# A small tile behind the others in its pool, and three pieces of a matmul stage in another order on the engines

## The chip, the cores and the metric

The kernel runs on one core of one Trainium2 chip. The time is device time of one launch in microseconds (us), the median of several runs. Five engines work side by side: PE (TensorE, matmuls; its weight loads are shown as PEld), DVE (VectorE), ACT (ScalarE), POOL (GpSimd) and SP, which here only issues DMAs.

## The reference

Three pieces follow one another. Attention over pooled keys and values gives 4608 tokens of 512 features; a gated layer (1536 wide) gives 4608 x 512 again; the last one, the **rational stage**, is the one that is changed:

```python
h = x @ w_in                                  # 4608x512 @ 512x2048
P = a[0] + a[1]*h + a[2]*h**2 + a[3]*h**3
Q = 1.0 + abs(b[0])*abs(h) + abs(b[1])*h**2
g = P / (Q + 1e-06)
return g @ w_out                              # 4608x2048 @ 2048x512
```

Everything is fp32. A product of two fp32 matrices is made of three matmuls on "high" and "low" parts (high x high, low x high, high x low).

## The kernel before

**Tiling.** The tokens are cut into 9 blocks of 512. The 2048 hidden columns are taken 256 at a time: a **couple** `n` is one block `j` and one of its 8 pairs `c` of 128 columns, so there are 72 couples (`TOTAL`), `n = 8j + c`. For a couple PE makes `z` (the hidden values, two PSUM banks of 128x512: `z_gv`, the left half, and `z_at`, the right half), ACT and DVE turn `z` into `g = P/Q`, and 24 matmuls of 128x512 (`out2`, profile line L1217, tile `acco`) add `g @ w_out` into four result banks, one for each 128 tokens. Here `g` is the stationary operand, loaded 128x128 at a time, and a tile of `w_out` (`wo`) moves.

**Two ways to make z.** Blocks 0 to 2 (couples 0 to 23, "plain") use 24 matmuls of 128x512 (`whole`, L262). Blocks 3 to 8 ("seven") use a seven-product scheme with 42 matmuls of 128x256 (`product`, L1182), spread over two turns of the loop (`begin7`).

**From z to g.** For a half (or for both halves at once, `all_`) the steps are: `look` (three ACT reads of z: L1252, L1255, L1258), `denominator` (DVE, L1272), `inverse` (ACT, Ln and Exp: L1278, L1279), `poly` (two DVE operations that read z again: L1267, L1268; after them the bank of z is free), `quotient` (DVE, L1283, L1284), `finish` (DVE, L1288), `high` (ACT rounds to the high part of g, L1308) and `low` (the low part of g, on POOL at L1317 or on DVE at L96). `g` stands in tiles `g0` (high) and `g1` (low), three buffers each.

**Order.** The order on each engine is that of the code; nothing is rescheduled. Turn `n` of the loop makes z of couple `n`, does the second part of the chain for couple `n-1`, and issues `outputs(n-3, 1)` and later `outputs(n-2, 0)`: result rows 2, 3 of couple `n-3`, and rows 0, 1 of couple `n-2`. Couple 0 and the last one, 71, are carried through the chain in one go by `alone(n)`. A waiting instruction holds what stands behind it on its engine.

**Banks and tiles.** z has two `gv` and two `at` banks, so z of couple `n` waits for `poly` of couple `n-2`. The result banks are the four of a ring: a block's results are copied out by `leave2` to a tile `ob` (two buffers) and sent with a DMA: row 0 (DVE), row 1 and row 3 (ACT) in turn `c == 2` of the next block, row 2 (DVE) in turn `c == 3`. The block's new rows 2 and 3 are begun in that same turn.

**The pool.** SBUF tiles of the stage come from a pool `p2`, one after another in the order in which the code first asks for them. The first is

```python
turn_ = p2.tile([P, 8], F32, name="turn")
```

32 bytes in a partition; it is written by a one-column copy on POOL that only keeps POOL in its place in the order. Behind it stand `sq`, `w0`, `t`, `g0`, `g1`, `ob`, `cq`, whose sizes are whole multiples of 1024 bytes. In the built program the first buffer of `g` begins at byte 198432 of a partition (32 above a multiple of 64), as all of `p2` behind `turn` does; the weights of all other 128x512 matmuls begin at multiples of 64.

Of the kernel before, what the change touches and what calls it, by code (L numbers as in the profile page):

```python
# [10 lines left out]
F32 = mybir.dt.float32  # L11
# [8 lines left out]
P = 128  # L20
# [4 lines left out]
DM = H * D  # L25
# [4 lines left out]
BLK = 512  # L30
# [36 lines left out]
def attention_gated_rational(  # L67
# [4 lines left out]
    nc = tc.nc  # L72
# [1056 lines left out]
    with tc.tile_pool(name="p2", bufs=1, reuse_waits="tile") as p2:  # L1129
# [11 lines left out]
        def seven(n):  # L1141
            return n // NC2 >= PLAIN2
# [25 lines left out]

        def zbanks(n):
            zs[n] = [  # L1170
                pool.tile([P, BLK], F32, tag=tag, name=f"z{n}_{tag}") for pool, tag in ((ps_gv, "gv"), (ps_at, "at"))
            ]

        Q_C11, Q_C12, Q_C21, Q_C22 = range(4)
# [33 lines left out]
        def out2(n, half):  # L1208
            j, c = divmod(n, NC2)
            if c == 0:  # L1210
                for i in (0, 1) if half == 0 else (2, 3):
                    accs[j, i] = chain_bank(f"acco{j}_{i}")
            gt = gts[n]
            for i in (0, 1) if half == 0 else (2, 3):
                for m, (lw, rw) in enumerate(((0, 0), (1, 0), (0, 1))):
                    for f in range(2):
                        nc.tensor.matmul(  # L1217
                            accs[j, i], gts[n][lw][:, f * BLK + i * P : f * BLK + (i + 1) * P],
                            W2[f"o2_{2 * c + f}"][:, rw, :],
                            start=c == 0 and m == 0 and f == 0, stop=c == NC2 - 1 and m == 2 and f == 1,  # L1220
                        )
            if half:
                gts.pop(n)

        def leave2(n, i, eng=None):
            j, c = divmod(n, NC2)
            if n < 0 or c < NC2 - 1:
                return
            ob = p2.tile([P, DM], F32, tag="ob", name=f"ob{j}_{i}", bufs=2)
            if eng is None:  # L1230
                nc.scalar.activation(ob, accs[j, i], AF.Copy)
            else:
                eng.tensor_copy(ob, accs[j, i])  # L1233
            r0 = j * BLK + i * P
            nc.sync.dma_start(out[r0 : r0 + P, :], ob)
# [29 lines left out]
        def poly(n, c):  # L1265
            t, z = tiles[n]["t"][:, c], zs[n][c.start // BLK]
            nc.vector.tensor_tensor(t, t, z, op=ALU.mult)  # L1267
            nc.vector.scalar_tensor_tensor(t, t, neg[:, 1:2], z, op0=ALU.add, op1=ALU.mult)  # L1268

        def denominator(n, c):  # L1270
            sq, w0 = tiles[n]["sq"][:, c], tiles[n]["w0"][:, c]
            nc.vector.scalar_tensor_tensor(w0, sq, neg[:, 5:6], w0, op0=ALU.mult, op1=ALU.add)  # L1272
# [14 lines left out]
            e, t = (tiles[n][k][:, c] for k in ("e", "t"))  # L1287
            nc.vector.scalar_tensor_tensor(e, t, neg[:, 0:1], e, op0=ALU.add, op1=ALU.mult)  # L1288

        def alone(n):  # L1290
            denominator(n, left)
            inverse(n, left)
            if not seven(n):
                poly(n, left)
            denominator(n, right)
            inverse(n, right)
            poly(n, right)
            quotient(n, left)
            finish(n, left)
            high(n, left)  # L1300
            quotient(n, right)
            finish(n, right)
            high(n, right)
            low(n, left)
            low(n, right)

        def high(n, c):
# [81 lines left out]

        counts = {}  # L1390
        sums2 = {}

        def sum_begin(n):
            c = n % NC2
# [31 lines left out]
        for n in range(EARLY2):  # L1426
            stream2(n)
        left, right = cols[True]
        turn_ = p2.tile([P, 8], F32, name="turn")

        def outputs(n, half):
            if 0 <= n < TOTAL:
# [2 lines left out]
        for n in range(TOTAL):  # L1435
            after = n + 1 if n + 1 < TOTAL and seven(n + 1) else None
            j, c = divmod(n, NC2)
            chain_tiles(n)
            x_load(n)
            if seven(n):  # L1440
                product(n, Q_C11, "a12", "b21")
                product(n, Q_C12, "s4", "b22")
                product(n, Q_C21, "s3", "t3")
                stream2(n + 2, 0, 1)
                add7(n, Q_C22)
                look(n, left)
                if seven(n - 1):
                    inverse(n - 1, all_)
                poly(n, left)
            else:  # L1450
                whole(n, 0)
                look(n, left)
                whole(n, 1)
                sum_begin(n)
                held.pop(n)
                stream2(n + EARLY2, *((0, 1, 3, 2) if seven(n + EARLY2) else ()))
            leave2(n - 3, 0, nc.vector)
            leave2(n - 4, 2, nc.vector)
            if after:
                begin7(after)  # L1460
            leave2(n - 3, 1)
            if seven(n):
                x_high(n, X_HIGH[c])
            elif j + 1 < PLAIN2:
                if "x" in box:
                    box.pop("x")()
            else:
                x_do(n, X_POOL[c], nc.vector)
                x_do(n, X_DVE[c], nc.vector)
            sum_low(n)  # L1470
            if n > 1:
                quotient(n - 1, all_)
            outputs(n - 3, 1)
            if seven(n):
                product(n, Q_C21, "a22", "t4")
                held.pop(n)
                stream2(n + 2, 3)
            if after:
                product(after, Q_C21, "s2", "t2")
                if seven(n):  # L1480
                    stream2(n + 2, 2)
            if n > 1:
                finish(n - 1, all_)
            if after:
                add7(after, Q_C12)
            look(n, right)
            if n > 1:
                high(n - 1, left)
                high(n - 1, right)
            if n == 0:  # L1490
                alone(n)
            elif n == TOTAL - 1:
                low(n - 1, all_, nc.gpsimd)
                alone(n)
            elif seven(n):
                poly(n, right)
                if X_POOL[c] and j + 1 < NB:
                    nc.gpsimd.tensor_copy(turn_[:, :1], tiles[n - 1]["e"][:, :1])  # L1498
                    x_do(n, X_POOL[c], nc.gpsimd)
                x_do(n, X_DVE[c], nc.vector)  # L1500
                denominator(n, all_)
                nc.gpsimd.tensor_copy(turn_[:, :1], tiles[n]["w0"][:, :1])  # L1502
                low(n - 1, all_, nc.gpsimd)
            else:
                denominator(n, all_)
                if n > 1:
# [12 lines left out]
            outputs(n - 2, 0)  # L1519
# [63 lines left out]
```

## Time and profile before

| | |
|---|---|
| three runs | 1759.24, 1759.27, 1761.99 us; median 1759.27 |
| the profiled execution | 1762.16 us; its span, first to last instruction, 1760.3 us |
| PE busy | 1720.0 us (98%) |
| weight loads (PEld) busy | 1441.5 us (82%) |
| DVE, ACT, POOL busy | 1357.8 (77%), 1156.6 (66%), 590.1 us (34%) |
| the rational stage | from 974.92 us to the end |

Busy shares tell how much an engine had to do; since PE's matmuls overlap one another, 98% does not mean that PE could not go faster. What sets the time is read from the order of events: which engine waits for which.

### The profile page before, as it was taken

The page shows a single profiled execution, that of the slowest core. Times are in us where ns is not written, and L with a number is a line of the kernel's source. Part 1 is how long each engine was busy: PE and PEld are TensorE (multiplying, and loading weights), DVE is VectorE, ACT ScalarE, POOL GpSimd, SP SyncE. Part 2 cuts the span into 40 slices and gives each one's busy share as a digit, 9 for nine tenths or more (in the row PEclk, how much of TensorE's full clock was granted, in tenths as well). Part 3 has the DMA queues.
Part 4 walks back from the last instruction along what each step waited for, and adds up shares of the span by engine and source line. Part 5 has one row for each costly group of instructions (what it writes and reads, how often), then busy time and mean ns, then how long its engine had stood idle before and what let it go on. Part 6 is the DMA issues. An engine that isn't in the chain of part 4 may idle for free.

```text
span 1760.3 us, 26293 instructions
## 1 busy us (share of the span) xinstructions
PE 1720.0 (98%) x9040; PEld 1441.5 (82%) x9040; DVE 1357.8 (77%) x2030; ACT 1156.6 (66%) x1980; POOL 590.1 (34%) x685
## 2 busy tenths in 40 slices
PE   6999999999999999999999999999999999999998
PEld 5777787788777888788888788888888888898887
DVE  7996767678677664387777799997888888888887
ACT  6785557577577654355545677776677777777775
POOL 3443334344635532100000164542343333333321
PEclk9999999999999999999999999999999999999999
DMA  7833767889999999994527545445446464555540
GB/s 286 296 137 135 252 250 247 314 327 379 380 325 356 335 335 354 386 394 168 192 80 255 192 168 191 168 156 202 154 165 254 154 233 172 218 191 198 190 176 25
DMA packets 173924, 413.11 MB, mean 235 GB/s; under 512 B 16864, under 2 KB 71008, under 8 KB 172768
## 3 DMA queue, kind: packets, MB, share of 16 engines
q1 hardware_dynamic: 172928, 410.85, 64.3%
q8 instruction: 72, 1.18, 0.3%
q10 hardware_dynamic: 864, 0.60, 0.1%
q14 instruction: 60, 0.49, 0.1%
HBM read 307.57 MB, written 103.81 MB: 234 GB/s over the span
## 4 chain that ended last, share of the span: by engine, by line
PE 82%; DVE 7%; ACT 5%; issue 2%; POOL 2%; DMA 1%; POOLq 0%; SPq 0%; DVEq 0%; ACTq 0%
PE acco L1217 22%; PE ca L262 10%; PE z_at L1182 9%; PE ya L1110 7%; PE cc L262 5%; PE z_gv L1182 4%; PE yc L1110 4%; PE z_gv L262 3%; PE z_at L262 3%; PE vp L262 3%; PE gp L262 3%; PE cb L262 2%; PE yb L1110 2%; PE pv L463 2%; PE sc L374 1%
## 5 line engine op out<-in xcount | busy, mean ns | idle before, releaser
L1217 PE MATMUL acco<-wo,g 128*128 128x512 f32 x1728 | 423.7, 395 | 3.8 <-DVE ob L1233 2.9
L1217 PEld LDWEIGHTS acco<-wo,g 128*128 128x128 f32 x1728 | 317.1, 188 | 75.3 <-DVE ob L1233 5.6
L1317 POOL TENSOR_TENSOR g<-e,g 128x512 fp32r<-128x512 f32 x140 | 190.3, 1381 | 390.1 <-PE z_at L262 284.8
L1252 ACT ACTIVATE t<-z_gv,neg 128x512 f32<-128x512 f32 x72 | 56.0, 777 | 100.7 <-PE z_gv L1182 73.4
L1272 DVE SCALAR_TENSOR_TENSOR w<-sq,neg,w 128x1024 f32<-128x1024 f32 (+1 forms) x74 | 95.1, 1286 | 21.1 <-ACT w L1258 21.1
L1283 DVE SCALAR_TENSOR_TENSOR e<-w,sq 128x1024 f32<-128x1024 f32 (+1 forms) x74 | 92.1, 1244 | 24.9 <-ACT sq L1279 22.3
L1308 ACT ACTIVATE g<-e 128x512 fp32r<-128x512 f32 x144 | 83.6, 630 | 41.3 <-DVE e L1288 40.6
L262 PE MATMUL vp<-x,wv 128*128 128x512 f32 x432 | 109.8, 402 | 0.7 <-DVE wv L96 0.4
L262 PE MATMUL gp<-x,wg 128*128 128x512 f32 x432 | 106.8, 394 | 1.4 <-DVE wg L96 0.9
L1288 DVE SCALAR_TENSOR_TENSOR e<-t,neg,e 128x1024 f32<-128x1024 f32 (+1 forms) x74 | 95.8, 1295 | 2.6
L262 PEld LDWEIGHTS gp<-x,wg 128*128 128x128 f32 x432 | 79.8, 188 | 20.4 <-DVE wg L96 2.9
L262 PEld LDWEIGHTS vp<-x,wv 128*128 128x128 f32 x432 | 80.1, 190 | 19.5 <-DVE wv L96 2.8
L1284 DVE SCALAR_TENSOR_TENSOR e<-e,sq 128x1024 f32<-128x1024 f32 (+1 forms) x74 | 91.9, 1241 | 2.5
L1252 ACT ACTIVATE t<-z_at,neg 128x512 f32<-128x512 f32 x72 | 56.2, 781 | 49.6 <-PE z_at L1182 37.9
L1279 ACT ACTIVATE sq<-sq,lnb 128x1024 f32<-128x1024 f32 (+1 forms) x74 | 83.6, 1130 | 2.4
L1278 ACT ACTIVATE sq<-w 128x1024 f32<-128x1024 f32 (+1 forms) x74 | 77.1, 1042 | 9.2 <-DVE w L1272 8.9
L1267 DVE TENSOR_TENSOR t<-t,z_gv 128x512 f32<-128x512 f32 x72 | 49.3, 685 | 32.6 <-ACT w L1258 32.6
L126 POOL TENSOR_TENSOR rawo<-rawo 128x256 uint32<-128x256 uint32 (+1 forms) x41 | 32.0, 781 | 120.1 <-issue 34.6
L941 DVE TENSOR_TENSOR cc<-cq,ca 128x512 f32<-128x512 f32 x36 | 25.0, 694 | 59.9 <-PE ca L262 59.9
L1502 POOL COPY turn<-w 128x1 f32<-128x1 f32 x47 | 8.7, 185 | 162.9 <-DVE w L1272 152.4
L262 PE MATMUL z_gv<-z,y 128*128 128x512 f32 x252 | 60.8, 390 | 1.5 <-DVE t L1268 1.5
L1498 POOL COPY turn<-e 128x1 f32<-128x1 f32 x35 | 6.5, 185 | 165.6 <-DVE e L1288 165.6
(361 smaller groups left out, 4433.8 us busy)
## 6 DMA issues: line engine op xcount, KB each, us to landing
y<-s2d SPq DMA_DIRECT2D x98, 512.0 KB, 4.9
y<-i_parts SPq DMA_DIRECT2D x91, 512.0 KB, 5.9
sw<-sd SPq DMA_DIRECT2D x72, 512.0 KB, 6.9
sw<-wd SPq DMA_DIRECT2D x36, 512.0 KB, 6.7
h<-hq SPq DMA_DIRECT2D x36, 512.0 KB, 6.8
y<-i_parts SPq DMA_DIRECT2D x49, 256.0 KB, 3.2
sd<-ws SPq DMA_DIRECT2D x24, 512.0 KB, 3.2
hl<-h SPq DMA_DIRECT2D x24, 512.0 KB, 6.7
```

Source lines behind the costliest of these rows:

```text
L262: nc.tensor.matmul(acc, st[:, lw, cols], mv[:, rw, mcols], start=first and i == 0, stop=last and i == n - 1, skip_group_check=seeded,)
L1110: nc.tensor.matmul(banks[q], w[:, lw, cols], t[:, rw, :], start=opened and k == 0 and m == 0, stop=k == NK - 1 and m == 2, skip_group_chec ...
L1182: nc.tensor.matmul(zpart(n, q), w[:, lw, (2 * k + i) * P : (2 * k + i + 1) * P], t[rw][i], start=first and m == 0, stop=m == 5, skip_group ...
L1217: nc.tensor.matmul(accs[j, i], gts[n][lw][:, f * BLK + i * P : f * BLK + (i + 1) * P], W2[f"o2_{2 * c + f}"][:, rw, :], start=c == 0 and m ...
L1252: nc.scalar.activation(tiles[n]["t"][:, c], zs[n][c.start // BLK], AF.Identity, scale=neg[:, 3:4], bias=neg[:, 2:3])
L1272: nc.vector.scalar_tensor_tensor(w0, sq, neg[:, 5:6], w0, op0=ALU.mult, op1=ALU.add)
L1279: nc.scalar.activation(ln, ln, AF.Exp, scale=-1.0, bias=lnb)
L1283: nc.vector.scalar_tensor_tensor(e, w0, C1, ln, op0=ALU.add, op1=ALU.mult)
L1284: nc.vector.scalar_tensor_tensor(e, e, 2.0, ln, op0=ALU.subtract, op1=ALU.mult)
L1288: nc.vector.scalar_tensor_tensor(e, t, neg[:, 0:1], e, op0=ALU.add, op1=ALU.mult)
L1308: nc.scalar.activation(gts[n][0][:, c], tiles[n]["e"][:, c], AF.Copy)
L1317: eng.tensor_tensor(lo[:, h], e[:, h], f32(hi[:, h]), op=ALU.subtract)
```

## The change

Four edits, all in the rational stage.

1. The 32-byte tile `turn` is asked for when it is first used, and so stands behind all other tiles of `p2`. In the built program the first buffer of `g` then begins at byte 198400, a multiple of 64.
2. Start: couple 0 puts its left half into an `at` bank and its right half into a `gv` bank. `alone(0)` is gone: couple 0 gets `denominator`, `inverse` and both `poly` in its own turn, and the second part of its chain in turn 1, behind couple 1's `look`.
3. The copy of result row 2 (`leave2(n-4, 2)`) goes ahead of `poly(n, left)` on DVE.
4. End: `last_couple` takes the place of `alone(71)`; it weaves the second part of couple 70's chain into that of couple 71, with `low(70)` on DVE. In all couples the matmuls with the low part of `g` come last of the three; in couple 71 all rows take the left half of g first, then the right. The last four results leave through four tiles.

```diff
-                pool.tile([P, BLK], F32, tag=tag, name=f"z{n}_{tag}") for pool, tag in ((ps_gv, "gv"), (ps_at, "at"))
+                pool.tile([P, BLK], F32, tag=tag, name=f"z{n}_{tag}")
+                for pool, tag in ((ps_gv, "gv"), (ps_at, "at"))[:: 1 if n else -1]
...
-            for i in (0, 1) if half == 0 else (2, 3):
-                for m, (lw, rw) in enumerate(((0, 0), (1, 0), (0, 1))):
-                    for f in range(2):
...
+            rows = (0, 1) if half == 0 else (2, 3)
+            steps = [(i, m, f) for i in rows for m in range(3) for f in range(2)]
+            if n == TOTAL - 1:
+                steps = [(i, m, half) for i in range(4) for m in range(3)]
+            for i, m, f in steps:
+                lw, rw = ((0, 0), (0, 1), (1, 0))[m]
...
+            if n < TOTAL - 1:
+                ob = p2.tile([P, DM], F32, tag="ob", name=f"ob{j}_{i}", bufs=2)
+            else:
+                ob = p2.tile([P, WIDE], F32, tag=("sq", "w0")[i // 2], name=f"ob{j}_{i}", bufs=2)[:, :DM]
...
+        def last_couple(n):
+            look(n, right)
             inverse(n, left)
+            for h in (left, right):
+                finish(n - 1, h)
+                high(n - 1, h)
             denominator(n, right)
             inverse(n, right)
+            for h in (left, right):
+                low(n - 1, h)
             quotient(n, left)
             finish(n, left)
             high(n, left)
+            poly(n, right)
+            low(n, left)
             quotient(n, right)
             finish(n, right)
             high(n, right)
-            low(n, left)
             low(n, right)
...
-        turn_ = p2.tile([P, 8], F32, name="turn")
...
+        def turn(src):
+            if not turns:
+                turns.append(p2.tile([P, 8], F32, name="turn"))
+            nc.gpsimd.tensor_copy(turns[0][:, :1], src[:, :1])
...
                 add7(n, Q_C22)
+                leave2(n - 4, 2, nc.vector)
                 look(n, left)
...
                 poly(n, left)
+                if n == TOTAL - 1:
+                    denominator(n, left)
...
-            leave2(n - 4, 2, nc.vector)
...
-            if n > 1:
-                quotient(n - 1, all_)
+            if n == 1:
+                look(n, right)
+            if n > 0:
+                for h in (left, right) if n == 1 else (all_,):
+                    quotient(n - 1, h)
+                    if n == 1:
+                        finish(n - 1, h)
...
             if n == 0:
-                alone(n)
+                for h in (left, right):
+                    denominator(n, h)
+                    inverse(n, h)
+                poly(n, left)
+                poly(n, right)
             elif n == TOTAL - 1:
-                low(n - 1, all_, nc.gpsimd)
-                alone(n)
+                last_couple(n)
```

**Start, DVE.** These are DVE's rows for couple 0 and the first of couple 1, before (`w`, `t`, `e`, `g` are the tiles of the chain; the first numbers of a couple's tiles are 95xx and 96xx).

```order
L1272 SCALAR_TENSOR_TENSOR w_9586<-sq_9585,neg,w_9586 128x512
L1267 TENSOR_TENSOR t_9587<-t_9587,z_gv 128x512
L1268 SCALAR_TENSOR_TENSOR t_9587<-t_9587,neg,z_gv 128x512
L1272 SCALAR_TENSOR_TENSOR w_9586<-sq_9585,neg,w_9586 128x512
L1267 TENSOR_TENSOR t_9587<-t_9587,z_at 128x512
L1268 SCALAR_TENSOR_TENSOR t_9587<-t_9587,neg,z_at 128x512
...
L1288 SCALAR_TENSOR_TENSOR e_9629<-t_9587,neg,e_9629 128x512
L96 SCALAR_TENSOR_TENSOR g_9628<-e_9629,g_9627 128x512 x2
L1272 SCALAR_TENSOR_TENSOR w_9650<-sq_9649,neg,w_9650 128x1024
```

And of the change:

```order
L1277 SCALAR_TENSOR_TENSOR w_9585<-sq_9584,neg,w_9585 128x512 x2
L1272 TENSOR_TENSOR t_9586<-t_9586,z_at 128x512
L1273 SCALAR_TENSOR_TENSOR t_9586<-t_9586,neg,z_at 128x512
L1272 TENSOR_TENSOR t_9586<-t_9586,z_gv 128x512
L1273 SCALAR_TENSOR_TENSOR t_9586<-t_9586,neg,z_gv 128x512
...
L1293 SCALAR_TENSOR_TENSOR e_9628<-t_9586,neg,e_9628 128x512
L1277 SCALAR_TENSOR_TENSOR w_9639<-sq_9638,neg,w_9639 128x1024
L96 SCALAR_TENSOR_TENSOR g_9627<-e_9628,g_9626 128x512 x2
```

Both denominators now stand ahead of both polynomials, and couple 1's denominator ahead of couple 0's low part. On ACT, `high` of couple 0 moved from before the six reads of couple 1's z to behind them.

**A block's fourth turn, DVE** (the one of block 3; `ob_2` is the copy of result row 2), before:

```order
L1206 TENSOR_TENSOR z_at<-cq_11959,z_at 128x256
L1267 TENSOR_TENSOR t_12029<-t_12029,z_gv 128x512
L1268 SCALAR_TENSOR_TENSOR t_12029<-t_12029,neg,z_gv 128x512
L1233 COPY ob_2_12063<-acco_2_11274 128x512
L1283 SCALAR_TENSOR_TENSOR e_12058<-w_11907,sq_11906 128x1024
```

And of the change:

```order
L1207 TENSOR_TENSOR z_at<-cq_11959,z_at 128x256
L1238 COPY ob_2_12053<-acco_2_11273 128x512
L1272 TENSOR_TENSOR t_12029<-t_12029,z_gv 128x512
L1273 SCALAR_TENSOR_TENSOR t_12029<-t_12029,neg,z_gv 128x512
L1288 SCALAR_TENSOR_TENSOR e_12061<-w_11907,sq_11906 128x1024
```

The copy moved up past two operations. This is so at six places, in blocks 3 to 8; in blocks 1 and 2 nothing stood between on DVE, and its rows are as before.

**The end, DVE** (tiles 16xxx and 17034, 17035 are couple 70's, 17009, 17010 and higher couple 71's), before:

```order
L1288 SCALAR_TENSOR_TENSOR e_17035<-t_16910,neg,e_17035 128x1024
L1272 SCALAR_TENSOR_TENSOR w_17009<-sq_17008,neg,w_17009 128x512 x2
L1267 TENSOR_TENSOR t_17010<-t_17010,z_at 128x512
L1268 SCALAR_TENSOR_TENSOR t_17010<-t_17010,neg,z_at 128x512
L1283 SCALAR_TENSOR_TENSOR e_17071<-w_17009,sq_17008 128x512
...
L1288 SCALAR_TENSOR_TENSOR e_17071<-t_17010,neg,e_17071 128x512
L96 SCALAR_TENSOR_TENSOR g_17070<-e_17071,g_17069 128x512 x2
```

And of the change:

```order
L1293 SCALAR_TENSOR_TENSOR e_17035<-t_16910,neg,e_17035 128x512 x2
L1277 SCALAR_TENSOR_TENSOR w_17009<-sq_17008,neg,w_17009 128x512
L96 SCALAR_TENSOR_TENSOR g_17034<-e_17035,g_17033 128x512 x2
L1288 SCALAR_TENSOR_TENSOR e_17066<-w_17009,sq_17008 128x512
L1289 SCALAR_TENSOR_TENSOR e_17066<-e_17066,sq_17008 128x512
L1293 SCALAR_TENSOR_TENSOR e_17066<-t_17010,neg,e_17066 128x512
L1272 TENSOR_TENSOR t_17010<-t_17010,z_at 128x512
L1273 SCALAR_TENSOR_TENSOR t_17010<-t_17010,neg,z_at 128x512
L96 SCALAR_TENSOR_TENSOR g_17065<-e_17066,g_17064 128x512
```

Couple 70's low part came to DVE (POOL loses its two last subtractions), couple 71's left denominator went up in front of couple 70's quotient, and couple 71's right polynomial moved behind its left quotient.

## Rows read from the trace of the kernel before

**Rows 1.** Chain that ended last, merged: start us, us, engine, tile, line, count

```profile
843.67 8.16 PE yc L1110 x36
...
1009.91 2.73 PE z_at L262 x12
1012.63 5.59 PE acco L1217 x24
...
1023.68 5.59 PE acco L1217 x24
...
1248.72 2.79 PE acco L1217 x12
...
1259.30 2.79 PE acco L1217 x12
1270.64 2.79 PE acco L1217 x12
```

**Rows 2.** Busy us by stretch of one couple: PE, PEld, DVE, ACT, POOL, clock, DMA

```profile
1023.67:1034.72 11.05, 11.05 (x50) 9.02 (x49) 10.95 (x11) 7.14 (x12) 9.04 (x7) 1.00 0.29 118
...
1200.39:1211.44 11.05, 11.05 (x50) 9.01 (x49) 8.82 (x10) 7.47 (x11) 3.10 (x2) 1.00 0.15 51
```

**Rows 3.** What PE waited for in the rational stage: us, times, longest

```profile
PE acco L1217 <- DVE ob L1233: 2.9, 6, 0.5
```

**Rows 4.** Timeline at the stage's start: start us, us, [idle before <-releaser]

```profile
974.92 3.02 PE L262 MATMUL z_gv<-z,wi 128*128 128x512 f32 x12 [0.69 <-ACT yq L1079]
...
982.58 0.75 DVE L1272 SCALAR_TENSOR_TENSOR w<-sq,neg,w 128x512 f32<-128x512 f32 x1 [0.59 <-ACT w L1258]
...
985.94 2.88 PE L262 MATMUL z_gv<-z,wi 128*128 128x512 f32 x12
...
989.51 0.76 ACT L1252 ACTIVATE t<-z_gv,neg 128x512 f32<-128x512 f32 x1
...
991.38 2.96 PE L1217 MATMUL acco<-wo,g 128*128 128x512 f32 x12
...
993.11 1.28 DVE L1272 SCALAR_TENSOR_TENSOR w<-sq,neg,w 128x1024 f32<-128x1024 f32 x1 [2.77 <-ACT w L1258]
...
995.83 3.03 PE L262 MATMUL z_gv<-z,y 128*128 128x512 f32 x12 [1.49 <-DVE t L1268]
```

**Rows 5.** Timeline, fourth turn of block 3

```profile
1265.43 0.69 DVE L1267 TENSOR_TENSOR t<-t,z_gv 128x512 f32<-128x512 f32 x1 [0.73 <-ACT w L1258]
1265.51 1.56 PE L1217 MATMUL acco<-wo,g 128*128 128x512 f32 x6
...
1266.82 0.68 DVE L1233 COPY ob<-acco 128x512 f32<-128x512 f32 x1
...
1267.56 1.66 PE L1217 MATMUL acco<-wo,g 128*128 128x512 f32 x6 [0.49 <-DVE ob L1233]
```

**Rows 6.** The tile ob: its DMAs, from issue to landing

```profile
DMA to landing us min/median/max: 2.0/2.1/5.9
```

**Rows 7.** Timeline at the end

```profile
1737.92 1.23 DVE L1283 SCALAR_TENSOR_TENSOR e<-w,sq 128x1024 f32<-128x1024 f32 x1 [0.66 <-ACT sq L1279]
1737.92 6.84 PE L1217 MATMUL acco<-wo,g 128*128 128x512 f32 x27
1738.12 0.78 ACT L1252 ACTIVATE t<-z_at,neg 128x512 f32<-128x512 f32 x1 [0.24 <-PE z_at L1182]
...
1742.47 2.98 POOL L1317 TENSOR_TENSOR g<-e,g 128x512 fp32r<-128x512 f32 x2 [5.57 <-ACT g L1308]
...
1744.35 1.65 DVE L1283 SCALAR_TENSOR_TENSOR e<-w,sq 128x512 f32<-128x512 f32 x1
...
1745.50 10.77 PE L1217 MATMUL acco<-wo,g 128*128 128x512 f32 x45 [0.74 <-POOL g L1317]
...
1747.42 0.68 DVE L1283 SCALAR_TENSOR_TENSOR e<-w,sq 128x512 f32<-128x512 f32 x1
...
1756.35 0.69 DVE L1233 COPY ob<-acco 128x512 f32<-128x512 f32 x1 [2.16 <-PE acco L1217]
```

More of the change, by code (lines that the diff above doesn't have):

```diff
@@ L1212, in out2 @@
                     accs[j, i] = chain_bank(f"acco{j}_{i}")
-            gt = gts[n]
-            for i in (0, 1) if half == 0 else (2, 3):
-                for m, (lw, rw) in enumerate(((0, 0), (1, 0), (0, 1))):
-                    for f in range(2):
[L1217 to L1221, printed above, removed]
+            rows = (0, 1) if half == 0 else (2, 3)
[4 more added lines that the diff above has]
+                lw, rw = ((0, 0), (0, 1), (1, 0))[m]
+                nc.tensor.matmul(
+                    accs[j, i], gts[n][lw][:, f * BLK + i * P : f * BLK + (i + 1) * P], W2[f"o2_{2 * c + f}"][:, rw, :],
+                    start=c == 0 and m == 0 and f == 0, stop=c == NC2 - 1 and m == 2 and f == 1,
+                )
             if half:
@@ L1228, in leave2 @@
                 return
-            ob = p2.tile([P, DM], F32, tag="ob", name=f"ob{j}_{i}", bufs=2)
+            if n < TOTAL - 1:
+                ob = p2.tile([P, DM], F32, tag="ob", name=f"ob{j}_{i}", bufs=2)
+            else:
+                ob = p2.tile([P, WIDE], F32, tag=("sq", "w0")[i // 2], name=f"ob{j}_{i}", bufs=2)[:, :DM]
             if eng is None:
@@ L1288, in finish @@
             nc.vector.scalar_tensor_tensor(e, t, neg[:, 0:1], e, op0=ALU.add, op1=ALU.mult)
-        def alone(n):
-            denominator(n, left)
+        def last_couple(n):
+            look(n, right)
             inverse(n, left)
-            if not seven(n):
-                poly(n, left)
+            for h in (left, right):
+                finish(n - 1, h)
+                high(n - 1, h)
             denominator(n, right)
             inverse(n, right)
-            poly(n, right)
+            for h in (left, right):
+                low(n - 1, h)
             quotient(n, left)
@@ L1391, in attention_gated_rational @@
         sums2 = {}
+        turns = []
+        def turn(src):
+            if not turns:
+                turns.append(p2.tile([P, 8], F32, name="turn"))
+            nc.gpsimd.tensor_copy(turns[0][:, :1], src[:, :1])
         def sum_begin(n):
@@ L1449, in attention_gated_rational @@
                 poly(n, left)
+                if n == TOTAL - 1:
+                    denominator(n, left)
             else:
                 whole(n, 0)
+                leave2(n - 4, 2, nc.vector)
                 look(n, left)
@@ L1481, in attention_gated_rational @@
                     stream2(n + 2, 2)
-            if n > 1:
+            if 1 < n < TOTAL - 1:
                 finish(n - 1, all_)
@@ L1485, in attention_gated_rational @@
                 add7(after, Q_C12)
-            look(n, right)
-            if n > 1:
+            if 1 != n < TOTAL - 1:
+                look(n, right)
+            if 0 < n < TOTAL - 1:
                 high(n - 1, left)
@@ L1497, in attention_gated_rational @@
                 if X_POOL[c] and j + 1 < NB:
-                    nc.gpsimd.tensor_copy(turn_[:, :1], tiles[n - 1]["e"][:, :1])
+                    turn(tiles[n - 1]["e"])
                     x_do(n, X_POOL[c], nc.gpsimd)
@@ L1501, in attention_gated_rational @@
                 denominator(n, all_)
-                nc.gpsimd.tensor_copy(turn_[:, :1], tiles[n]["w0"][:, :1])
+                turn(tiles[n]["w0"])
                 low(n - 1, all_, nc.gpsimd)
@@ L1505, in attention_gated_rational @@
                 denominator(n, all_)
-                if n > 1:
+                if n == 1:
+                    low(n - 1, left)
+                    low(n - 1, right)
+                else:
                     low(n - 1, all_, nc.gpsimd)
```

## The prediction

> **What bounds the kernel now.** I read the chain of waits first, then busy time by stretch, then what PE waited for, and last the order of events at the three places that the change touches. In the rational stage the chain is PE nearly without a break, and each plain couple follows the last after 1023.68 - 1012.63 = 11.05 us, in which PE has no gap [rows 1]. A heavy couple (DVE 10.95 us, POOL 9.04) and a light one (DVE 8.82, POOL 3.10) take the same 11.05 us at the same granted clock of 1.00 [rows 2]. So the other engines only matter where PE waits for one: the reader should see three such places, the first couples, the six block changes, and the last two couples. All else must come from the pace of the matmuls themselves.
>
> That pace is not one number. 36 matmuls of the layer before take 8.16 us, 226.7 ns each; 12 for z take 2.73 us, 227.5 ns; but 24 of `acco` take 5.59 us, 232.9 ns [rows 1]. All are 128x512 of the same type, in the same couple as the z ones, and neither the clock nor the neighbours' load differs [rows 2]. What I see that differs is the place of the stationary operand: g starts 32 bytes above a multiple of 64, all other such weights at one.
>
> **Edit 1, the small tile.** It moves g by 32 bytes and adds no instruction; the other tiles of the pool move too, on engines that PE doesn't wait for. The trace before has no `acco` matmul with g at a multiple of 64, so the price is bounded: nothing at the one end; at the other the pace of the neighbours, 5.59 - 24 x 0.2267 = 0.15 us a couple, over 72 couples 10.8 us. I take the upper end, because every 512-column group whose weights start at a multiple of 64 runs near 227 ns and the only one that doesn't runs at 233. Why 32 bytes should cost this no row tells; it is a coincidence of two facts that I take for a cause.
>
> The Trainium skill speaks against it: its page "SBUF — State Buffer", section "Specifications (TRN2)", gives SBUF lines of 16 bytes and a penalty for crossing to a new one. 32 is a whole number of such lines, so by that rule g was as well placed before as after, and edit 1 is worth nothing. The same page says in "Operand start alignment" that its alignment runs timed nothing. No run here yet shows which holds; the sum by that rule is the first rival below.
>
> **Edit 2, the start.** Before, z of couple 0 waits 0.69 us for the copy of the last `ya` out of the `gv` bank. With the left half in `at` it starts at 974.2; the right half needs that bank 2.7 us later. Next, couple 3's z starts at 995.83, 1.49 us late by the profile, for couple 1's polynomial; couple 1's reads began only at 989.51, since ACT stood behind couple 0's `high`, and DVE idled 2.77 us before couple 1's denominator at 993.11 [rows 4]. After: couple 0's right denominator at 981.85 (0.7 earlier than 982.58), then four polynomial operations at about 0.72 each, so the `gv` bank that couple 2 wants is free at 985.4, half a microsecond ahead of 985.94. Couple 2's 24 matmuls end at 990.9. DVE meanwhile runs without a gap: six operations for quotient and finish of couple 0 to 989.8, couple 1's denominator (1.28) to 991.1, two low parts to 992.5, couple 1's left polynomial to 994.0. PE's 12 matmuls of couple 0's rows start at 990.9, need the low part 1.1 us in, wait some 0.4 us, and end at 994.0. Couple 3's z starts there: 995.83 - 994.0 = **1.8 us**. Bounds: 0.7 (the bank alone) and 2.4 (no new wait). DVE has come forward by about as much, so the lead lasts.
>
> **Edit 3, row 2's copy.** Couples of the seven-product part follow one another after 1259.30 - 1248.72 = 10.58 us, but over the block change 1270.64 - 1259.30 = 11.34 [rows 1]: 0.76 us more, at six block changes 4.5 us. The cause stands in the rows: after six matmuls from 1265.51 the bank of the next row is still being copied, from 1266.82 to 1267.50 [rows 5], and the waits list the same copy six times [rows 3]. In its new place DVE meets the copy at about 1264.7, in the 0.73 us for which it idles for ACT's reading [rows 5]; the copy takes 0.68. So it is hidden, ends 1.5 us before PE asks, and the polynomial behind it is at most some hundredths late. Without that cover it would cost 0.68 us of DVE, on which PE doesn't wait there. Gain **4.5 us**; the lower bound is the idle time as recorded, 2.9 [rows 3].
>
> **Edit 4, the end.** From 1737.92 PE has 27 matmuls at 0.233, 6.29 us, then should go on at 1744.21; it goes on at 1745.50, having waited for POOL's low part of couple 70 (from 1742.47 for 2.98 us) [rows 7]. That is 1.3 us. After it the last 45 run through. In the new order, from DVE's 1737.92: couple 70's quotient 2.5 us, then fifteen operations of 0.72 (0.68 by the row at 1747.42, and the step to the next): finish twice, denominator, low part of 70 at the fifth (1744.0), quotient, finish, polynomial and low part left at the eleventh (1748.3), low part right at the fifteenth, some 1752.0 with its wait for ACT's rounding. POOL no longer works beside DVE, which had stretched one of these to 1.65 us [rows 7]. PE at 226.7 ns asks for these at 1744.3, 1749.3 and 1752.0: in time, the last by a hair. The order of the three terms alone (low last) only gives each low part two more matmuls of time. So 1.3 us; against it the four results come out 0.68 us apart instead of 1.4, and four transfers of 256 KB that land after 2.1 us when alone [rows 6] may queue: 0.2 us by guess. Gain **1.1 us**, bounds 0.3 and 1.6. The copy and the DMA behind the last matmul (1756.35 to the end) stay.
>
> **Sum.** 10.8 + 1.8 + 4.5 + 1.1 = 18.2 us. The profiled execution took 1762.16 (span 1760.3), so one like it would take 1744.0, with a span of 1742.1. The median run was 2.9 us shorter than the profiled one; from 1759.27 the forecast is **1741.1 us**, about 1.0% faster.
>
> **Rivals.**
> First, the pace stays: what slows `acco` is something that the change keeps, such as g having been written only just before by ACT and POOL, or two tiles of w_out by turns. Against it: z and the layer before also go through several moving tiles, and the pace is the same beside idle and busy neighbours. It is what the page's rule would give. Time: 1759.27 - 7.4 = 1751.9.
> Second, DVE takes PE's place as the bound in the plain blocks: a couple there would have 11.05 - 0.15 = 10.90 us and the heaviest DVE row is 10.95 [rows 2]. Light couples between give it back; if the gain of edit 1 were lost in all of the first 16 couples, 2.4 us, the time would be 1743.5.
> Third, slower: the copy of row 2 waits for its buffer of `ob`, that is, for the landing of row 1's DMA, and now holds the polynomial, and with it z's bank, behind it. It stands some 6.7 us after that DMA's issue; the longest landing was 5.9 [rows 6]. Beyond 6.7 each microsecond costs one at each of six places; to end 0.2% above before, landings would have to pass 10.3 us, a wait of 3.62 us six times, 21.7 against the 18.2 gained: 1762.8.
> That the change doesn't do what it says is no rival here: the order on the engines and the place of g are those of the built program.
>
> **How the numbers follow.** Forecast 0.74, with a range of its own from 1740.0 (start and end at their upper bounds, 19.3 us gained) to 1745.7 (edit 1 at 90%, the other three at their lower bounds, 13.6 gained). Pace stays 0.15; DVE the bound 0.04; edit 1 in part, between the first two, 0.02; the late landing 0.05, of which 0.02 costs enough to end above before by 0.2% and 0.03 eats the gain only. The range of 1739.0 to 1752.5 leaves a microsecond under the forecast's best case and takes in the first rival's centre, without which a fifth of the chance would hang on one unproved cause. A run of this kernel tells 0.2% (3.5 us) from no change; faster by more has 0.95, within it 0.03, slower 0.02.
>
> **What would show it.** In the chain, 24 `acco` matmuls should take 5.44 us, plain couples follow after 10.90 and the others after 10.43, block changes too. If 5.59 stays, edit 1 was worth nothing. No wait of `acco` for `ob` should be left; couple 3's z should start near 994.0; behind the last z PE should run 72 matmuls with no gap over 0.1 us. I am wrong if PE shows new waits for a polynomial or a low part, above all in blocks 0 to 2, or if the last DMA lands much more than 2.2 us after its issue.

## The result, and the profile after

| | before | after |
|---|---|---|
| median | 1759.26 us (1759.05 to 1761.99, 4 runs) | 1745.26 us (1744.37 to 1747.41, 4 runs) |
| the profiled execution, its span | 1762.16, 1760.3 us | 1747.41, 1745.6 us |

The ratio is 0.9919, with a 95% interval of 0.9901 to 0.9936: 14.0 us less by the medians, where 18.2 were forecast. The time lies inside the range given, 4.2 us above the forecast's 1741.1. Between the two profiled executions, which the rest of this section compares, it is 14.7 us.

The chain of waits of the kernel after, in the plain blocks and in block 3 (start us, us, engine, tile, line, count):

```profile
988.08 2.72 PE z_at L262 x12
...
1009.92 5.44 PE acco L1220 x24
1020.80 5.44 PE acco L1220 x24
...
1242.74 2.75 PE acco L1220 x12
...
1253.26 2.75 PE acco L1220 x12
...
1263.78 2.75 PE acco L1220 x12
```

Read it against [rows 1]. The 24 `acco` matmuls take 5.44 us where they took 5.59, so they run at the pace of their neighbours, and a plain couple follows the last after 1020.80 - 1009.92 = 10.88 us. In the seven-product blocks a group of 12 takes 2.75, not 2.79, and a couple 1253.26 - 1242.74 = 10.52 us, block changes (1253.26 to 1263.78) too. The forecast had 10.43 there.

All that PE and its weight loads still wait for in the stage (us, times, longest); the first row is at couple 2's z, the second in couple 0's result rows:

```profile
PEld z_gv L262 <- DVE t L1273: 0.5, 1, 0.5
PEld acco L1220 <- DVE g L96: 0.2, 1, 0.2
```

The wait of `acco` for `ob` [rows 3] is gone. DVE is busy nearly throughout a heavy plain couple and PE still does not wait for it (busy us by stretch: PE, PEld, DVE, ACT, POOL, clock, DMA):

```profile
1023.36:1034.24 10.88, 10.88 (x49) 9.01 (x48) 10.74 (x11) 6.95 (x12) 9.29 (x6) 1.00 0.08 31
```

The three places in the timeline, in order (start, block 3's fourth turn, end):

```profile
973.96 2.88 PE L262 MATMUL z_at<-z,wi 128*128 128x512 f32 x12
...
993.42 2.90 PE L262 MATMUL z_gv<-z,y 128*128 128x512 f32 x12
...
1258.54 0.68 DVE L1238 COPY ob<-acco 128x512 f32<-128x512 f32 x1
...
1259.44 2.91 PE L1220 MATMUL acco<-wo,g 128*128 128x512 f32 x12
...
1724.34 16.51 PE L1220 MATMUL acco<-wo,g 128*128 128x512 f32 x72
...
1737.09 0.69 DVE L96 SCALAR_TENSOR_TENSOR g<-e,g 128x512 fp32r<-128x512 f32 x1 [0.70 <-ACT g L1316]
```

Couple 3's z starts at 993.42 (995.83 before, 994.0 forecast). The copy of row 2 is done at 1259.22, before PE comes to the bank. The last 72 matmuls are one piece without an idle stretch. The tile `ob` shows landings up to 4.6 us in the whole stage, and the last four alone up to 3.0:

```profile
DMA to landing us min/median/max: 2.0/2.0/4.6
...
DMA to landing us min/median/max: 2.0/2.0/3.0
```

Cut at the same events in both traces (each stretch from the start of one matmul to the start of the next one named), 14.6 of the 14.7 us by which the profiled spans differ lie here; the other 0.1 lies ahead of the stage:

| stretch | before | after | less | forecast |
|---|---|---|---|---|
| last `ya` matmul to couple 3's z | 21.99 | 19.69 | 2.30 | 1.8, and 0.1 of pace |
| from there to the first seven-product matmul (plain couples) | 226.52 | 223.06 | 3.46 | 3.2 |
| to couple 22's `acco` | 15.62 | 15.58 | 0.04 | |
| to couple 68's `acco` (46 couples, six block changes) | 491.52 | 483.92 | 7.60 | 4.5 and 6.9 |
| to the last z | 8.31 | 8.24 | 0.07 | |
| last z to the last `acco` matmul | 18.07 | 16.24 | 1.82 | 1.3, and 0.44 of pace |
| last `acco` matmul to the end | 4.47 | 5.14 | -0.67 | -0.2 |

Of the 7.60, 4.5 are the block changes; the other 3.1 are 0.067 us a couple, where 0.15 was forecast. Against the 18.2 forecast, that shortfall of 3.8 us and 0.5 at the very end were missed, and the other stretches together gave some 0.8 more than forecast: 3.5 us net. The medians are 4.2 off because the forecast was carried over from the profiled execution, which stood 2.9 us over the median before and 2.15 after.

### The profile page after: what moved, and what is told of

Same layout as the page of the kernel before. It is cut to its first block, busy times and chain, and to the rows that moved or that the text cites. A ratio compares the mean times of both kernels' runs of the same rounds, so it can differ in the third digit from the quotient of the medians.

```text
span 1745.6 us, 26288 instructions
## 1 busy us (share of the span) xinstructions
PE 1710.6 (98%) x9040; PEld 1443.4 (83%) x9040; DVE 1357.4 (78%) x2033; ACT 1156.9 (66%) x1980; POOL 586.9 (34%) x683
## 4 chain that ended last, share of the span: by engine, by line
PE 85%; DVE 5%; ACT 4%; issue 2%; POOL 2%; DMA 2%; SPq 0%; DVEq 0%; POOLq 0%; ACTq 0%
PE acco L1220 23%; PE z_at L1183 10%; PE ca L262 10%; PE ya L1110 7%; PE cc L262 5%; PE z_gv L1183 4%; PE z_gv L262 4%; PE yc L1110 4%; PE z_at L262 4%; PE vp L262 3%; PE gp L262 3%; PE cb L262 2%; PE yb L1110 2%; PE pv L463 2%; PE sc L374 1%
## 5 line engine op out<-in xcount | busy, mean ns | idle before, releaser
L1220 PE MATMUL acco<-wo,g 128*128 128x512 f32 x1728 | 413.8, 390 | 0.0
L410 POOL TENSOR_TENSOR p<-p,sm 128x576 f32<-128x576 f32 (+1 forms) x36 | 44.5, 1237 | 49.5 <-DVE sm L409 39.8
L980 DVE TENSOR_TENSOR cq<-cq,ca 128x512 f32<-128x512 f32 x36 | 24.4, 677 | 47.1 <-PE ca L262 47.1
```

The costliest lines, as they stand in the source:

```text
L1220: nc.tensor.matmul(accs[j, i], gts[n][lw][:, f * BLK + i * P : f * BLK + (i + 1) * P], W2[f"o2_{2 * c + f}"][:, rw, :], start=c == 0 and m ...
```

## The experiments

Two questions are open after this: what sets the pace of `acco`, and why it gives back only about half as much in blocks 3 to 8. The edits are told apart on the way.

**One edit at a time, added to the kernel before.** `turn_only` has edit 1, `start_only` edit 2, `copy_only` edit 3 and `end_only` edit 4 (with the four tiles of the last results). Of each, the lines at its core:

```diff
turn_only
-        turn_ = p2.tile([P, 8], F32, name="turn")
+                turns.append(p2.tile([P, 8], F32, name="turn"))
copy_only
+                leave2(n - 4, 2, nc.vector)
                 look(n, left)
start_only
+                for pool, tag in ((ps_gv, "gv"), (ps_at, "at"))[:: 1 if n else -1]
...
+                for h in (left, right) if n == 1 else (all_,):
end_only
-                low(n - 1, all_, nc.gpsimd)
-                alone(n)
+                last_couple(n)
```

> The kernel before with edit 1 alone, the small tile behind the others. Theory (the place of g): plain couples follow after 10.88 us, the other couples after 10.52, block changes still with 0.75 us of wait; 3.4 + 3.1 us less than before, about 1752.7. Rival (the pace came with the new order of the matmuls or of the engines): 5.59 us for 24 acco matmuls as before, time as before, 1759.3. The forecast on record, without a second limit, would give 10.8 us less, 1748.5.

> The kernel before with edit 3 alone, row 2's copy ahead of the left polynomial in blocks 3 to 8. Theory (one wait of 0.75 us at each of six block changes, hidden under DVE's idle time): 4.5 us less, 1754.8, no wait of acco for ob, couples 10.59 us throughout. Rival (the wait moves to a polynomial or the next bank): under 2 us less.

> The kernel before with edit 2 alone, the first couple's banks and order. Theory (the lead lasts): couple 3's z starts 2.1 us earlier against the last ya than before, and the time is 2.1 us less, 1757.2. Rival (the lead is given back by DVE in the heavy plain couples): PE shows waits for a low part or a polynomial in blocks 0 to 2, and the time is within 0.7 us of before.

> The kernel before with edit 4 alone, the last couple and the order of the three terms. Theory (a stall of 1.3 us goes, and the four results leave in a row so that the last lands some 0.7 us later): 0.6 us less, 1758.7, from the last z to the last acco matmul 16.7 us against 18.07, from there to the end 5.1 against 4.47. Rival (the order of the terms matters in all couples): couples other than 11.05 and 10.59 us.

| kernel | median us | kernel before | ratio, 95% interval |
|---|---|---|---|
| `turn_only` | 1753.02 | 1759.36 | 0.9965 (0.9953 to 0.9978) |
| `copy_only` | 1755.12 | 1759.59 | 0.9976 (0.9966 to 0.9985) |
| `start_only` | 1758.11 | 1759.59 | 0.9996 (0.9987 to 1.0005) |
| `end_only` | 1758.96 | 1759.59 | 0.9998 (0.9989 to 1.0007) |

The chain of `turn_only`, and what its PE waited for at the block changes:

```profile
1020.46 5.44 PE acco L1217 x24
...
1242.40 2.75 PE acco L1217 x12
...
1252.92 2.75 PE acco L1217 x12
```

```profile
PE acco L1217 <- DVE ob L1233: 3.0, 6, 0.5
```

The tile's place alone gives 5.44 and 2.75, with no instruction added or moved in time. So the first rival falls; the medians differ by 6.3 us. The Trainium skill's page "SBUF — State Buffer" ("Specifications (TRN2)") gives lines of 16 bytes, from which the prediction drew that a move by two whole lines is worth nothing; for these operands that does not hold. But `turn_only` also gives 2.75 only, so the shortfall is in edit 1 itself and not in what the others do to it.

`copy_only` loses the six waits for `ob` and its couples follow after 10.59 us throughout, 4.5 us less. `start_only` reaches couple 3's z 20.15 us after the last `ya` matmul (21.99 before): 1.84 us; the prediction had 1.8, the expectation of this run 2.1. Its PE still waits for the low part of couple 0:

```profile
989.33 1.93 PEld L1218 LDWEIGHTS acco<-wo,g 128*128 128x128 f32 x9 [0.42 <-DVE g L96]
```

`end_only` takes 16.68 us from the last z to the last `acco` matmul (18.07): 1.39, forecast 1.3, but 5.24 from there to the end (4.47). The medians of these two lie within what their intervals call no change; their sizes are read from the traces.

**Edit 1 taken out of the kernel after.** `turn_first` asks for the small tile first again:

```diff
     with tc.tile_pool(name="p2", bufs=1, reuse_waits="tile") as p2:
+        first_ = p2.tile([P, 8], F32, name="turn")
...
-        turns = []
+        turns = [first_]
```

> The changed kernel with edit 1 undone: the small tile first, all else new. Theory (the place of g): plain couples after 11.05 us, others after 10.59, no wait at the block changes; 6.6 us over the changed kernel, about 1751.9. Rival (the pace hangs on the order): 10.88 and 10.52 us, 1745.3.

1751.99 us (before 1759.36, ratio 0.9962, 0.9949 to 0.9975), 6.7 above the kernel after, with 5.59 and 2.79 in the chain. Edit 1 is worth about the same with and without the others (6.7 and 6.3).

**Is it the multiple of 64?** `g_aligned` puts 32 more bytes ahead of g in that kernel, so that g begins at a multiple of 64 that is no multiple of 256:

```diff
+            if n == 0:
+                p2.tile([P, 8], F32, name="gap")
             gts[n] = [p2.tile([P, WIDE], F32R, tag=f"g{i}", name=f"g{i}{n}", bufs=3) for i in range(2)]
```

> The changed kernel with the small tile first and another of 32 bytes right ahead of g, so that g starts at a multiple of 64 again (an odd one) while sq, w0 and t stay 32 bytes off. Theory (the weights' place alone): as the changed kernel, 1745.3, 24 acco matmuls in 5.44 us in plain couples. Rival (the place of the tiles that ACT, DVE and POOL work on): as with edit 1 undone, 1751.9.

1752.75 us (ratio 0.9959, 0.9946 to 0.9973); its chain:

```profile
1021.41 5.60 PE acco L1221 x24
...
1232.00 2.80 PE acco L1221 x12
```

The expectation of 1745.3 was missed and the rule "a multiple of 64" falls. In the built programs g begins 64 bytes above a multiple of 256 here, 32 above one in the kernel before, and at one in the kernel after; the moving `wo` begins at multiples of 256 in all of them, and in every other fp32r matmul of 128x512 in these programs both operands do.

**TensorE alone.** Two kernels time groups of fp32r matmuls like those of `acco`, with no other engine at work; only the width and where the weights `w` and the moving operand `m` begin are changed. (The expectations call the seven-product blocks "six-product".)

```python
c = off // 4 + (k % 8) * P
x = moff // 4 + (k % 2) * 512
nc.tensor.matmul(bank[:, :cols], w[:, c : c + P], m[:, x : x + cols], ...)
```

> This kernel leaves out the whole computation: PE alone runs groups of fp32r matmuls with no other engine at work, and only fills the output. Groups of 48 matmuls of 128x512 whose weights start 0, 16, 32, 48, 64 and 96 bytes above a multiple of 128; one with the moving operand 32 bytes off; groups of 128x256 at 0 and 32; and 12 of 128x512 behind 30 or 6 of 128x256, by turns. Theory (the place of the weights): 226.7 ns a matmul at 0 and 64, 233 ns at 32 and 96, the moving operand's place free. Rival (the pace of acco had another cause, such as g just written): all groups at 226.7 ns. For the six-product blocks, where after the change 12 acco matmuls take 2.75 us in place of 2.72: if the slow first five matmuls (233, 236, 229, 232, 231 ns) come from the 256-column matmuls ahead of them, they show here too behind 30 of them; if they come from the other engines' work, all twelve take 226.7 ns.

> The computation is left out again; PE alone. Weights from 0 to 384 bytes above a multiple of 128 at a moving operand at 0; the moving operand at 16, 64, 128 with the weights at 0 and with the weights at the same offset; and for 32 pairs of offsets (256-column weights, 512-column weights) the pattern of a six-product couple, 30 of 256 columns, 12 of 512, 12 of 256, 12 of 512, twice. Theory (what counts is how far the weights lie from the moving operand, modulo 128 bytes): 0, 4 to 16, 128, 256 and 384 at 226.7 ns; 32 to 112 and 160, 192, 320 at 231 to 234; equal offsets of both always at 226.7. Rival (each operand's own place counts): equal offsets of 16 and 64 are slow, about 233. In the pattern: 10.52 us a turn at (0, 0) as in the changed kernel; if the slow head hangs on the place too, some pair comes near 10.43; if it comes from the change of width alone, none is under 10.50.

The chain of the first one (48 matmuls of 512 columns, or 96 of 256; the name tells the offset in bytes of the weights, `mthirtytwo` that of the moving operand, `both` 32 for the two; `half` and `halfoff` are the narrow ones with the weights 0 and 32 off; `la` are 12 of 512 columns behind 30 of 256):

```profile
102.63 10.88 PE wzero L34 x48
113.51 10.89 PE wsixteen L34 x48
124.40 11.19 PE wthirtytwo L34 x48
...
146.79 11.19 PE wsixtyfour L34 x48
...
169.22 11.20 PE mthirtytwo L34 x48
180.42 10.92 PE both L34 x48
191.34 11.52 PE half L34 x96
202.85 11.35 PE halfoff L34 x96
...
234.86 2.75 PE la L34 x12
```

Weights 32 or 64 bytes off cost 11.19 - 10.88 = 0.31 us in 48; so does the moving operand 32 bytes off; with both off by 32 the cost is gone but for 0.04. So what counts here is where the one stands against the other, and the expectation that the moving operand's place is free, and 64 as good as 0, was wrong. The narrow matmuls go the other way: 96 of them take 11.52 us with equal offsets and 11.35 with the weights 32 off. And `la` takes 2.75 with both at 0, as in blocks 3 to 8: the slower head (the first matmuls of a group) comes behind narrow matmuls without the rest of the kernel. By the starts in the trace those twelve run 234, 236, 228, 232 and 231 ns apart, then 227. A change of width is not needed for such a head: in the second kernel a 512-wide group with the weights 256 off, behind one with 192, runs 235, 229, 232 and 231 ns apart before it settles at 227. The kernel before had one too: in its `vp` group at 184.55, behind the attention scores, the matmuls from the second on follow one another after 231, 236, 228, 232 and 231 ns, then 227.

The second one takes more distances. Rows of its chain, 36 matmuls each, and the pattern of the seven-product blocks (30 of 256 columns, 12 of 512, 12 of 256, 12 of 512) in the places (0, 0) and (64, 64) for the weights of the narrow (`s`) and the wide (`l`) ones; `m` moves the moving operand alone, `b` both by the same:

```profile
102.23 8.17 PE wzero L34 x36
110.39 8.37 PE wfour L34 x36
...
127.07 8.41 PE wsixteen L34 x36
...
160.65 8.40 PE wthirtytwo L34 x36
169.04 8.40 PE wsixtyfour L34 x36
...
210.79 8.37 PE woneeight L34 x36
...
227.56 8.25 PE woneninetytwo L34 x36
235.81 8.18 PE wtwofiftysix L34 x36
243.99 8.40 PE wthreetwenty L34 x36
...
269.09 8.39 PE bsixteen L34 x36
277.49 8.26 PE msixtyfour L34 x36
...
293.91 8.36 PE moneeight L34 x36
302.27 8.17 PE boneeight L34 x36
310.44 3.60 PE szerozero L34 x30
320.96 3.59 PE szerozero L34 x30
...
732.34 3.40 PE ssixtyfoursixtyfour L34 x30
735.75 2.79 PE lsixtyfoursixtyfour L34 x12
738.54 1.37 PE ssixtyfoursixtyfour L34 x12
...
742.70 3.41 PE ssixtyfoursixtyfour L34 x30
```

256 is as 0 and 320 as 64; the moving operand 64 up is as the weights 192 up, and 128 either way is alike. So for most places the distance counts modulo 256 bytes, not 128 as was expected, and equal is fastest at 512 columns. The rule does not cover small offsets: the weights 4 bytes off are slow (8.37) where a fast pace was expected, 120 is as fast as 0 (8.17), both operands 16 off are slow (8.39) though the distance is 0, and the weights 16 off took 10.89 for 48, as 0 does, in the first kernel and 8.41 for 36 in the second, behind another group. So what ran just before can matter as well; why stays open. One turn of the pattern takes 320.96 - 310.44 = 10.52 us at (0, 0), exactly a couple of blocks 3 to 8 after, and 742.70 - 732.34 = 10.36 at (64, 64). There the wide groups are slower, 2.79 for 2.75, and the gain is the narrow ones', 3.40 for 3.59 and 1.37 for 1.43: by themselves they run faster away from the equal place. That 0.16 us was not tried in the kernel.

**Is it g, or what came along with it?** In every kernel so far with g at a multiple of 256 all the tiles of ACT, DVE and POOL stood at one too. `g_first` (made from `turn_first`) asks for the g tiles ahead of the small one, so that g begins at a multiple of 256 and all the others stay 32 bytes off:

```diff
+        early = [p2.tile([P, WIDE], F32R, tag=f"g{i}", name=f"g{i}0", bufs=3) for i in range(2)]
         first_ = p2.tile([P, 8], F32, name="turn")
```

> The kernel after with its g tiles as the first tiles of the pool and the small tile right behind them: g begins at a multiple of 256 bytes, as in the kernel after, and the other tiles (sq, w0, t, ob and the 1 KB cq), on which ScalarE, VectorE and GpSimd work, begin 32 bytes off, as in the kernel before. Theory (the distance between the weights g and the moving operand wo, modulo 256 bytes, sets TensorE's period): as the kernel after, 1745.3 us, acco matmuls 226.7 ns in the plain blocks, couples 10.88 and 10.52 us. Rival (the place of the tiles of the other engines sets it, and g came along with them): as with edit 1 undone, 1752.0 us, acco matmuls 233.2 ns, couples 11.05 and 10.59 us.

1744.08 us (1742.89 to 1745.23; before 1759.67, ratio 0.9908, 0.9894 to 0.9922), and the chain is that of the kernel after:

```profile
1029.22 5.44 PE acco L1222 x24
...
1240.28 2.75 PE acco L1222 x12
...
1250.80 2.75 PE acco L1222 x12
```

It is the place of g alone.

**The last outputs.** `tail_spread` is the kernel after with the last couple's matmuls in another order:

```diff
-                steps = [(i, m, half) for i in range(4) for m in range(3)]
+                order = ((0, 0), (1, 0), (2, 0)) if half == 0 else ((0, 1), (1, 1), (3, 0), (2, 1), (3, 1))
+                steps = [(i, m, f) for i, f in order for m in range(3)]
```

> The kernel after with the last couple's twelve steps in another order: left half rows 0, 1 and 2, then right half rows 0 and 1, left half row 3, right half rows 2 and 3, so that the four results are done further apart than one every 0.68 us. Theory (the last output lands late because the four follow one another so closely): the last transfer takes less than 3.03 us, last acco matmul to the end 4.5 us in place of 5.14, last z to last acco matmul unchanged at 16.2 us, so about 1744.7 us, 0.6 less than the kernel after, and that is below what the measurement can tell, so the trace decides. Rival (the last transfer is late for another reason, such as the queue that it is in): last acco matmul to the end stays 5.1 us, 1745.3 us.

1744.77 us (1743.64 to 1748.22; before 1759.67, ratio 0.9914, 0.99 to 0.9928), no difference from the kernel after that can be told. Its last output still landed 3.03 us after its issue, and the end came 5.14 us after the start of the last `acco` matmul; it spread the first three results but left 0.71 us between the last two. Meanwhile `g_first`, with all four 0.7 us apart as in the kernel after, landed its last in 2.06 and ended after 4.45 us. So the spacing, the prediction's reason, is not it. Two more runs: `last_ob` with the last two results in the buffers of `ob`, and the kernel after once more:

```diff
-            if n < TOTAL - 1:
+            if n < TOTAL - 1 or i > 1:
                 ob = p2.tile([P, DM], F32, tag="ob", name=f"ob{j}_{i}", bufs=2)
```

> The kernel after, but the last two of the four results leave through the two buffers of ob (in SBUF some 45 KB further up than the tiles sq and w0 that carry all four in the kernel after); when and on which engine each is copied and sent is as it was. With the four transfers 0.7 us apart the last one took 3.03 to 3.13 us in five kernels and 2.06 in the sixth, whose sq and w0 lie elsewhere in SBUF. Theory (the place of the tiles): the last lands 2.0 to 2.1 us after its issue and the last acco matmul to the end takes 4.45 us. Rival (the spacing, and the sixth was chance): 3.03 us again and 5.14. Elsewhere as the kernel after.

> The kernel after once more, unchanged. If the late landing of the last output (3.03 us) belongs to the kernel, it comes again and the last acco matmul to the end takes 5.14 us; if it is chance from one execution to the next, a landing near 2.05 us may come, with 4.45 us to the end.

`after_again` repeats the kernel after within a hundredth: 3.04 and 5.15 us (1747.8 us in that single run). `last_ob` (1743.34, single) answers neither way: all four landed in 2.46 to 2.86 us, the last in 2.70, and the end came 4.80 us after the last matmul. The queues show what goes along with it. DMA queues of the kernel after, from the last output's issue to its landing, then of `last_ob` around its first two outputs (queue, kind: packets, MB, share):

```profile
q1 hardware_dynamic: 333, 0.58, 49.5%
q14 instruction: 1, 0.01, 0.6%
```

```profile
q14 instruction: 1, 0.01, 0.7%
```

One packet of 8 KB of a queue whose kind is "instruction" goes between. In the kernel after it starts at 1743.29, takes 309 ns, and the last output packet starts right at its end, at 1743.60, when all others of that transfer are through. Where this packet falls orders every kernel here:

| the 8 KB packet starts | kernels | landing of the last output | last matmul to the end |
|---|---|---|---|
| behind the landing | before, `turn_only`, `copy_only`, `g_first` | 1.98 to 2.06 us | 4.24 to 4.47 us |
| 1.7 to 1.8 us after the last issue | after and its repeat, `turn_first`, `g_aligned`, `end_only`, `tail_spread` | 3.03 to 3.13 us | 5.14 to 5.24 us |
| 0.6 us after the last issue | `start_only` | 2.36 us | 4.52 us |
| 0.3 us before the last issue | `last_ob` | 2.70 us (all four 2.46 to 2.86) | 4.80 us |

In all twelve profiled executions the last output lands on time when this packet starts behind the landing, and late when it starts before. They go together without an exception, but that is no test: no run moved this packet alone, and what sets its moment was not tried. Nor does the packet account for all of it. In the kernel after the last output packet ends at 1743.70, 0.4 us behind the others, but the landing follows 0.94 us after that, where it follows after 0.35 in the kernel before; those 0.6 us are not explained.

## Why the prediction was right, and where it was off

**Edit 1** was the right term with a wrong price and a wrong rule. The pace of `acco` does hang on the place of g, against the first rival. That every 512-column group whose weights start at a multiple of 64 runs near 227 ns was true of the kernel before, heads of groups apart, only because those weights also start where their moving operand does, modulo 256; `g_aligned` and TensorE alone show that 64 is not enough. That the new place, 198400, is a multiple of 256 too was luck: at 64 bytes above one, as in `g_aligned`, this term would have given nothing. The size: plain blocks gave 3.46 us for 3.2 forecast. The step that failed is "over 72 couples": it took 5.59, the cost of 24 matmuls in a plain couple, for the seven-product blocks too, and the neighbours' 226.7 ns for what they could reach. There the `acco` matmuls come in groups of 12 behind narrow ones, whose first five run at 228 to 236 ns although g stands at the best place; TensorE alone shows the same head behind narrow matmuls. The 2.79 for such a group in [rows 1] is the same slow pace as the 5.59, so the rows did not tell the two cases apart, and no row of a fast 512-column group behind narrow ones was at hand; heads of groups that could have warned stood in the same trace, in the layer before. The measured gain is 0.067 us a couple instead of 0.15, about 3.8 us less in all.

**Edit 2** came as worked out: couple 3's z at 993.42 for 994.0, and in blocks 0 to 2 no wait beyond the two that the prediction had reckoned with, for couple 2's bank (0.5 us) and for couple 0's low part (0.2 for 0.4). The stretch gave 2.30 for 1.8. Edit 2 alone gave 1.84; that this equals the forecast is chance, for the forecast had the low part asked for 1.1 us into couple 0's rows, which is edit 4's order of the three terms. Without that order `start_only` waits 0.7 us there. With it, and with the old pace, `turn_first` takes 19.70 us, as the kernel after does (19.69), so the other 0.45 us belongs to the order and not to the pace.

**Edit 3** is exact: 4.5 us, alone and in the sum, with the copy hidden where DVE had been idle. The third rival, landings over 6.7 us, did not come; 4.6 was the longest.

**Edit 4**: the wait for POOL's low part was worth 1.39 us for 1.3, and the low parts came in time. The -0.2 for outputs close together was named as a guess. It measured -0.67, and the spacing is not the reason: outputs 0.7 us apart land in 2.06 us in `g_first`. The late landing goes along with the packet of the instruction queue; that the packet costs the 0.7 is likely and not shown.

**The second rival** fell: DVE has 10.74 us of work in a couple of 10.88, and PE shows no wait for it there.

**The sum**, from the traces: pace some 7.1, start 2.3, copies 4.5, end 1.39 - 0.67 = 0.7, together 14.6 of the 14.7 us.

## What to carry to other kernels

When matmuls of one shape run at two paces in one trace, write down where both operands begin and compare the distance modulo 256 bytes; here a tile of 32 bytes ahead of a pool cost the 512-column matmuls with their weights in that pool up to 3%. For narrow matmuls measure it apart; by themselves they ran faster away from the equal place. A pace taken from long groups of one shape is no price for short groups that alternate with another; price those from a row of the same alternation, or time TensorE alone. Where an end is late by a few tenths in some versions and not in others, look for foreign packets in the DMA queues before blaming one's own spacing.

## What the runs showed of the hardware that was not expected

- fp32r matmuls of 128x512: 226.7 ns apart with both operands at the same place modulo 256 bytes, about 233 with the weights 32, 64, 96, 160 or 320 bytes off (8.17 against 8.40 to 8.43 us for 36), between the two at 192 (8.25). Against that, 120 off is as fast as 0, and both operands 16 off are slow (8.39). Why is open.
- fp32r matmuls of 128x256 go the other way: 120 ns apart at the equal place, 118 with the weights 32 off (11.52 and 11.35 us for 96), 113 with the weights 64 off in the pattern at (64, 64) (3.40 us for 30).
- Behind a group of 256-column matmuls the first five of 512 columns run 228 to 236 ns apart with both operands at the same place; behind a 512-column group at another distance the first four did too. The pattern of the seven-product blocks took between 10.36 and 10.64 us a turn, by the places alone.
- In each of the eight (of twelve) profiled executions in which one 8 KB packet of the instruction queue started before the last 256 KB output had landed, that output was late, in six of them by about 1 us, though the packet takes 0.31 us only. That the packet is the cause was not tested.
